# A fused attention, gated-MLP and channel-mix kernel whose written-out instruction order is drawn up anew

## The chip, the cores and the metric

The kernel runs on one core of one Trainium2 chip. The metric is the device time of one execution in microseconds (us), lower is better. Times are of single executions; the profiled execution is one of them, with every instruction recorded.

## What is computed

Three layers follow each other, on 4 batches of 576 tokens:

```python
# attention: 8 heads of 64, with a decay from the running sum of log f
scores = q @ k.T / 8 + cum[:, None] - cum[None, :]      # causal
x = softmax(scores) @ v                                  # -> (4, 576, 512)
# gated MLP with a spatial product over the tokens
h = relu(x @ w_in); u, v = h[..., :512], h[..., 512:]
v = (v - mean) / sqrt(var + 1e-6)
x = (u * (w_spatial @ v + b_spatial)) @ w_out
# channel mix with the token before
k = relu((mu_k*x + (1-mu_k)*x_prev) @ w_k)
r = sigmoid((mu_r*x + (1-mu_r)*x_prev) @ w_r)
out = r * (k*k @ w_v)
```

## The kernel before

The work on the heads goes by pairs: pair p holds heads 2p and 2p+1 of the 32, so there are 16 pairs, four to a batch. A pair goes through these steps, each a method of class `K`:

- `load`, `qksq`, `qkscale`, `qkhi`, `qklo`: k and q are fetched, scaled and split into a high and a low half-precision part, and transposed by DMA into the tiles kT and qT. `kaux` and `qaux` copy half of them by DMA into kA and qA, where the decay rows are added.
- `score` (tiles s) and `rowmax`: the scores, for the row maxima alone. `mrow` sends the maxima through device memory (md) into two rows of qA.
- `scoreT` (tiles t): the scores again, transposed; ScalarE takes exp into the tile e, GpSimd zeroes the upper triangles (`causal`).
- `products`: `pv` multiplies e by v on 64-column groups of TensorE, `sums` adds e up on 32-column groups; all go to the one tile o in PSUM. `head` copies the numerators into xo.
- `recip`: the sums go to device memory (rd<-sm), come back reshaped (r<-rd), are inverted, and go out and back again (rd<-r, sr<-rd); `norm` multiplies xo by sr on GpSimd, `xhi` and `xlo` split the result into the tile xt of the pair.

When the four pairs of a batch b are there, the MLP of that batch runs: `m1v` (60 matmuls, x by the v half of w_in), `ln1` to `ln4` (normalising it, on ScalarE, VectorE and GpSimd), `m1u` (96 matmuls, the u half) and `m2` (112 matmuls, the spatial product; VectorE multiplies each of its 8 tiles into u, and a DMA sends it to device memory as gd). Each pass over an m1v tile ends with channel block kc = 3, which needs the xt of the batch's last pair. Weights are fetched and converted on the side (`wconv`, `wscale`, `wsplit` for w_in; `weights_spatial`; `early_blocks` for seven blocks of the later weights; `weights2` for the rest).

Then comes the channel mix on chunks of 512 tokens (`m3`, `mix`, `chunk`), a long run of matmuls. Its memory, and the last weights' fetches (mu, w_k, w_r, w_v), use space that the attention's tiles held, so they begin when pair 15 has finished.

All calls up to the last m2 are not issued at once. `Planned` records them, 4,209 in all, and `issue` sends them out in the order of the list `ORDER` (L36), as written in the file; each engine's queue is in that order, and nothing reorders it later. `SLOTS` (L216) fixes for some tiles which of a pool's buffers each use takes. The program that drew up the two tables is not in the file. In the profile L291 is the line of `issue`, so every recorded instruction has that line, and L305 is the line of the calls that come after it. All DMAs but three at the start are issued from one queue, that of SyncE (SP).

Of the kernel before, what the change touches and what calls it, by code (L numbers as in the profile page):

```python
# [36 lines left out]
    0, 2, 234, 1, 4, 961, 3, 6, 235, 5, 49, 7, 50, 51, 29, 99, 52, 53, 100, 101, 30, 40, 31, 233,  # L37
    41, 102, 103, 32, 245, 33, 253, 269, 277, 291, 301, 305, 34, 8, 9, 10, 11, 42, 12, 35, 69, 13, 14, 43,
    44, 36, 45, 57, 48, 17, 37, 15, 71, 54, 16, 18, 19, 38, 72, 59, 20, 55, 61, 21, 62, 22, 73, 46,
    63, 23, 26, 24, 28, 84, 25, 56, 39, 27, 60, 64, 85, 65, 74, 47, 86, 90, 91, 67, 87, 222, 92, 88,  # L40
    68, 95, 75, 93, 70, 89, 96, 108, 76, 58, 107, 109, 94, 66, 104, 78, 128, 79, 80, 110, 106, 111, 112, 81,
    113, 97, 114, 82, 77, 98, 138, 139, 115, 122, 105, 123, 124, 125, 126, 127, 132, 133, 141, 134, 130, 131, 129, 146,
    147, 142, 136, 218, 148, 149, 143, 144, 150, 186, 152, 232, 121, 153, 145, 154, 151, 155, 156, 157, 160, 158, 161, 162,
    268, 163, 159, 164, 165, 172, 168, 166, 169, 170, 294, 167, 171, 173, 174, 320, 175, 176, 391, 177, 179, 392, 137, 393,
    394, 395, 140, 396, 180, 184, 181, 188, 135, 397, 189, 187, 185, 223, 206, 178, 207, 190, 191, 192, 193, 182, 194, 199,
    183, 231, 219, 195, 200, 201, 202, 221, 203, 204, 205, 247, 214, 215, 216, 209, 196, 229, 248, 210, 197, 378, 249, 211,
    220, 250, 198, 83, 334, 212, 407, 319, 236, 251, 208, 386, 237, 238, 213, 255, 331, 256, 257, 217, 258, 259, 260, 224,
    225, 226, 239, 227, 240, 241, 252, 242, 261, 228, 243, 278, 279, 280, 262, 281, 244, 282, 283, 230, 263, 264, 310, 284,
    265, 266, 302, 303, 304, 286, 246, 267, 287, 285, 288, 289, 295, 290, 306, 270, 296, 311, 271, 312, 297, 292, 298, 293,
    299, 300, 313, 307, 308, 323, 324, 327, 314, 309, 332, 328, 329, 333, 325, 335, 317, 336, 337, 417, 330, 338, 339, 340,  # L50
    326, 343, 344, 345, 117, 116, 346, 341, 347, 348, 349, 416, 426, 350, 351, 342, 352, 315, 118, 353, 354, 355, 387, 356,
    357, 358, 119, 445, 380, 381, 382, 359, 383, 446, 384, 385, 360, 403, 447, 404, 405, 361, 389, 120, 415, 364, 448, 390,
    365, 515, 316, 449, 366, 408, 367, 450, 362, 368, 369, 272, 428, 423, 273, 429, 430, 525, 363, 451, 452, 453, 454, 425,
    455, 456, 274, 436, 467, 275, 457, 468, 469, 470, 495, 471, 276, 472, 458, 473, 321, 370, 371, 1151, 409, 474, 400, 398,
    401, 514, 505, 1152, 496, 475, 497, 498, 573, 372, 528, 519, 520, 522, 521, 501, 402, 580, 418, 388, 419, 420, 534, 421,
    535, 442, 406, 536, 537, 592, 506, 538, 539, 540, 437, 438, 524, 439, 422, 440, 507, 541, 574, 441, 575, 576, 424, 577,
    410, 578, 579, 459, 460, 499, 542, 461, 444, 462, 476, 477, 411, 478, 583, 479, 463, 412, 508, 484, 509, 584, 480, 510,
    485, 465, 322, 466, 486, 644, 481, 487, 482, 399, 488, 489, 670, 502, 503, 516, 517, 588, 589, 590, 443, 612, 601, 613,
    614, 504, 526, 518, 543, 527, 512, 544, 545, 689, 546, 593, 500, 523, 602, 628, 629, 630, 631, 632, 633, 615, 547, 548,
    706, 549, 581, 550, 551, 634, 552, 553, 611, 554, 555, 635, 556, 557, 558, 675, 749, 645, 646, 647, 511, 648, 649, 650,  # L60
    622, 413, 667, 668, 559, 669, 798, 623, 651, 560, 561, 414, 624, 799, 652, 564, 565, 625, 600, 800, 671, 683, 566, 626,
    801, 567, 676, 627, 568, 802, 569, 610, 677, 697, 570, 608, 571, 585, 694, 562, 586, 572, 678, 690, 254, 691, 679, 587,
    603, 744, 582, 604, 605, 680, 606, 464, 698, 563, 699, 607, 616, 617, 618, 2133, 803, 619, 318, 620, 636, 637, 638, 591,
    639, 2134, 483, 653, 609, 654, 804, 655, 656, 640, 692, 621, 700, 701, 693, 702, 703, 1153, 513, 657, 1154, 672, 704, 673,
    738, 739, 740, 674, 741, 742, 743, 705, 685, 686, 661, 771, 642, 687, 696, 643, 662, 772, 695, 663, 747, 658, 373, 664,
    374, 659, 665, 666, 748, 781, 753, 754, 755, 1155, 682, 375, 707, 681, 688, 708, 709, 594, 710, 763, 376, 711, 712, 745,
    713, 714, 715, 431, 716, 432, 717, 718, 719, 377, 720, 433, 721, 722, 734, 595, 770, 434, 735, 723, 750, 724, 751, 379,
    736, 596, 782, 783, 784, 597, 752, 807, 746, 808, 785, 809, 810, 811, 812, 773, 774, 725, 775, 813, 756, 776, 435, 780,
    786, 787, 788, 789, 814, 823, 777, 726, 824, 825, 826, 852, 827, 828, 845, 846, 790, 847, 792, 727, 829, 728, 779, 729,
    793, 830, 737, 730, 791, 731, 794, 427, 732, 733, 848, 795, 815, 853, 816, 778, 796, 875, 817, 762, 818, 831, 832, 833,  # L70
    819, 854, 834, 797, 868, 923, 869, 855, 598, 839, 835, 821, 856, 822, 840, 599, 491, 862, 836, 841, 857, 842, 490, 837,
    872, 764, 843, 844, 849, 850, 864, 865, 870, 851, 924, 876, 492, 866, 877, 878, 859, 879, 880, 945, 881, 867, 884, 871,
    885, 886, 493, 887, 888, 889, 890, 891, 892, 873, 882, 494, 893, 894, 874, 895, 896, 897, 898, 883, 899, 529, 917, 530,
    918, 919, 920, 921, 900, 922, 944, 931, 932, 531, 933, 901, 902, 926, 905, 954, 903, 906, 532, 907, 908, 904, 909, 927,
    910, 533, 971, 641, 972, 858, 936, 955, 765, 956, 957, 977, 978, 979, 980, 981, 953, 982, 757, 660, 758, 964, 943, 759,
    766, 999, 684, 760, 1000, 1001, 767, 1002, 1003, 1004, 911, 937, 912, 928, 913, 929, 983, 1156, 1157, 951, 761, 984, 1158, 925,
    946, 947, 948, 2375, 949, 1392, 930, 1028, 2376, 768, 1021, 1393, 1022, 1023, 1005, 950, 938, 965, 934, 966, 967, 769, 1006, 968,
    805, 939, 985, 952, 1024, 986, 940, 973, 987, 988, 1029, 1048, 969, 974, 916, 1030, 1049, 806, 1031, 935, 989, 1007, 970, 1008,
    1032, 1009, 1051, 1010, 1036, 1033, 1067, 991, 1068, 1069, 992, 1070, 1025, 1026, 975, 1055, 1015, 1011, 820, 941, 1052, 1016, 1027, 1017,
    860, 942, 1108, 1018, 914, 1019, 1020, 1012, 1045, 1046, 1104, 1013, 1071, 1105, 1130, 838, 1106, 1035, 1107, 1073, 1053, 1054, 1074, 1075,  # L80
    1047, 863, 958, 1076, 1072, 976, 1170, 1131, 1171, 1118, 1119, 1034, 1050, 1140, 1172, 1111, 1109, 990, 1077, 861, 1078, 1079, 1080, 1081,
    1082, 1112, 1083, 1084, 1085, 915, 1086, 1087, 1014, 1088, 1129, 1160, 1122, 1100, 959, 960, 1101, 1089, 962, 1037, 1115, 1090, 1116, 1102,
    1161, 1141, 963, 1162, 1142, 1117, 1166, 1167, 1110, 1168, 1169, 1132, 1133, 1145, 1134, 1091, 1139, 1135, 1120, 1146, 1147, 1148, 1136, 1163,
    1149, 1176, 1092, 1196, 1197, 1198, 1199, 1150, 1164, 1173, 1093, 1177, 1138, 1174, 1165, 1175, 1200, 1252, 1178, 1103, 1159, 1179, 1293, 1180,
    1181, 1202, 1121, 1203, 1189, 1201, 1204, 1205, 1232, 1233, 1190, 1290, 1191, 1182, 1192, 1193, 1209, 1206, 1194, 1184, 1195, 1185, 1235, 1236,
    1277, 1361, 1237, 1272, 1207, 1273, 1225, 1408, 1274, 1208, 1226, 1227, 1251, 1210, 1291, 1228, 1280, 1234, 1211, 1292, 1229, 1230, 1212, 1213,
    1295, 1238, 1245, 1244, 1214, 1246, 1239, 1247, 1215, 1248, 1257, 1249, 1362, 1216, 1250, 1217, 1266, 1258, 993, 1267, 1275, 1268, 1269, 1270,
    1259, 1271, 1276, 1261, 1283, 1284, 1260, 1123, 1285, 1289, 994, 1286, 1262, 1287, 1263, 1288, 1282, 1264, 1278, 1296, 1265, 1297, 1281, 1298,
    1308, 995, 1309, 1310, 1299, 1311, 996, 1312, 1313, 1316, 1240, 1350, 997, 1351, 1241, 1352, 1300, 1314, 1242, 1353, 1301, 1354, 1317, 1303,
    1355, 1407, 1315, 1356, 1302, 1357, 1360, 1358, 998, 1359, 1386, 1387, 1304, 1375, 1417, 1376, 1305, 1377, 1124, 1349, 1306, 1364, 1378, 1243,  # L90
# [1169 lines left out]
```

## Time and profile before

| | us |
|---|---|
| median of 3 runs (lowest to highest) | 718.86 (715.58 to 720.31) |
| the profiled execution | 720.54 |
| its span, first to last instruction | 718.8 |
| TensorE (PE) busy | 655.2 (91%) |
| weight loads (PEld) busy | 466.8 (65%) |
| VectorE (DVE) busy | 426.7 (59%) |
| ScalarE (ACT) busy | 372.1 (52%) |
| GpSimd (POOL) busy | 142.9 (20%) |

The span is read in stages: up to 24 us the first tiles are loaded and prepared; up to 112 us come pairs 0 to 4 with hardly any MLP work; up to 348 us attention and the MLPs of batches 0 to 2; up to 413 us the last products of attention and the MLP of batch 3; then the channel mix. TensorE's granted clock is given as a share of full speed, 1.00 for 2.4 GHz and 0.50 for 1.2 GHz.

### The profile page before, as it was taken

To read this page: it belongs to the slowest core of one execution; us is meant where nothing else is said; L and a number is where in the kernel's file an instruction comes from. 1 tells how busy PE (TensorE), PEld (TensorE's weight loads), DVE (VectorE), ACT (ScalarE), POOL (GpSimd) and SP (SyncE) were. 2 spreads that over 40 slices of the span, in tenths; PEclk is the share of its full clock that TensorE was granted. 3 is DMA by queue.
4 is the path that set the end of the run, shared out by engine and by line. 5 is a ranking of instruction groups with operands and counts; after the bars stand their busy time and mean duration, and the time that the engine had idled before them with its cause. 6 is when DMAs were issued, how large, how long until landed. Compare 5 with 4: busy or idle time off the path is not lost.

```text
span 718.8 us, 11708 instructions
## 1 busy us (share of the span) xinstructions
PE 655.2 (91%) x4238; PEld 466.8 (65%) x4238; DVE 426.7 (59%) x1077; ACT 372.1 (52%) x765; POOL 142.9 (20%) x343
## 2 busy tenths in 40 slices
PE   0598988999889999999858899999999999999997
PEld 0254544667545775557525687888888888888896
DVE  6778869896848946533139789465135413632351
ACT  5568857873678705564137478363236224532431
POOL 7023436501356303460115000000000000000000
PEclk9999979999999999999969999999999999999999
DMA  6887858646578324201133644011010100100010
GB/s 207 222 206 217 209 111 208 199 95 171 156 169 197 74 97 94 68 25 35 51 106 117 197 143 138 30 30 59 1 45 0 59 0 16 51 9 1 1 59 29
DMA packets 73615, 70.06 MB, mean 97 GB/s; under 512 B 50883, under 2 KB 51555, under 8 KB 73558
## 3 DMA queue, kind: packets, MB, share of 16 engines
q1 hardware_dynamic: 73126, 68.14, 35.2%
q10 hardware_dynamic: 432, 1.18, 0.5%
q8 instruction: 33, 0.54, 0.3%
q14 instruction: 24, 0.20, 0.1%
HBM read 43.78 MB, written 9.79 MB: 75 GB/s over the span
## 4 chain that ended last, share of the span: by engine, by line
PE 63%; DVE 12%; DMA 10%; ACT 5%; POOL 5%; issue 3%; SPq 2%; DVEq 0%; POOLq 0%; ACTq 0%
PE m L305 40%; PE m1u L291 4%; PE o L291 4%; PE s L291 4%; PE m L291 4%; PE t L291 4%; PE m1v L291 3%; SPq L291 2%; DMA sr<-rd 2%; ACT e L291 2%; DVE nm L291 2%; DMA wst<-in_moe_w_k_dram 1%; POOL xo L291 1%; POOL mv L291 1%; DVE wf L291 1%
## 5 line engine op out<-in xcount | busy, mean ns | idle before, releaser
L305 PE MATMUL m<-xx,moe_w_k 128*128 128x512 f32 (+1 forms) x480 | 105.5, 369 | 0.0
L305 PE MATMUL m<-moe_w_v,k 128*128 128x512 f32 x432 | 104.0, 390 | 0.0
L305 PEld LDWEIGHTS m<-xx,moe_w_k 128*128 128x128 f32 x480 | 84.0, 188 | 16.1
L305 PEld LDWEIGHTS m<-moe_w_v,k 128*128 128x128 f32 x432 | 80.7, 188 | 17.0
L291 ACT ACTIVATE e<-t,qa 128x512 f32<-128x512 f32 (+1 forms) x128 | 71.0, 593 | 28.8 <-PE t L291 20.9
L291 POOL TENSOR_SCALAR_AFFINE_SELECT e<-e 128x128 f32<-128x128 f32 (+1 forms) x160 | 54.5, 361 | 141.4 <-ACT e L291 141.1
L305 DVE TENSOR_TENSOR tmp<-tmp 128x512 f32<-128x512 f32 (+1 forms) x40 | 25.4, 638 | 94.1 <-ACT tmp L305 93.9
L291 PE MATMUL m1v<-win,xt 128*128 128x512 f16 x240 | 60.9, 397 | 12.0 <-ACT xt L291 11.2
L291 PE MATMUL s<-kT,qT 128*128 128x192 f16 (+3 forms) x192 | 55.1, 297 | 17.1 <-DMA qT<-nq 7.4
L305 ACT ACTIVATE tmp<-m 128x512 f32<-128x512 f32 (+1 forms) x40 | 22.3, 557 | 79.2 <-PE m L305 78.6
L305 PE MATMUL m<-gh,moe_w_out 128*128 128x512 f32 (+1 forms) x240 | 55.8, 382 | 2.8 <-DVE u L291 2.0
L291 DVE CUSTOM_DVE_ANT_0 junk<-s,mask 128x512 bf16<-128x512 f32 (+4 forms) x100 | 47.4, 474 | 13.5 <-PE s L291 9.9
L291 PE MATMUL m1u<-xt,win 128*128 128x288 f16 x384 | 52.6, 292 | 2.1 <-ACT u L291 2.1
L291 PE MATMUL m<-wspT,vn 128*128 128x288 f16 x384 | 53.3, 286 | 0.2 <-DVE wspT L291 0.2
L291 PE MATMUL s<-kA,qA 67*128 67x192 f16 (+3 forms) x192 | 49.4, 298 | 4.3 <-DMA qA<-qT 4.3
L305 PEld LDWEIGHTS m<-gh,moe_w_out 128*128 128x128 f32 x240 | 43.3, 193 | 12.8 <-DVE u L291 2.3
L291 PE MATMUL o<-e,v 128*64 128x64 f32 (+4 forms) x384 | 50.3, 397 | 1.4 <-ACT xo L291 0.7
L291 PE MATMUL t<-qA,kA 69*128 69x512 f16 (+2 forms) x192 | 48.5, 288 | 3.1 <-ACT e L291 2.7
L305 PE MATMUL m<-moe_w_r,xx 128*128 128x512 f32 x216 | 51.2, 394 | 0.0
L291 PE MATMUL t<-qT,kT 128*128 128x512 f16 (+2 forms) x192 | 50.1, 286 | 0.0
L291 PEld LDWEIGHTS <-xt 128*128 128x128 f16 x240 | 23.0, 101 | 39.6 <-ACT xt L291 11.7
L305 PEld LDWEIGHTS m<-moe_w_r,xx 128*128 128x128 f32 x216 | 40.4, 187 | 9.9
(162 smaller groups left out, 1087.4 us busy)
## 6 DMA issues: line engine op xcount, KB each, us to landing
knat<-in_k_dram SPq DMA_DIRECT2D x16, 320.0 KB
v<-in_v_dram SPq DMA_DIRECT2D x20, 256.0 KB
sr<-rd SPq DMA_DIRECT2D x32, 144.0 KB
gd<-u SPq DMA_DIRECT2D x16, 288.0 KB
out_dram<-o SPq DMA_DIRECT2D x18, 256.0 KB
qnat<-in_q_dram SPq DMA_DIRECT2D x14, 320.0 KB
wst<-in_moe_w_k_dram SPq DMA_DIRECT2D x8, 512.0 KB
g<-gd SPq DMA_DIRECT2D x16, 256.0 KB
```

The lines of the kernel that those rows point to most:

```text
L291: self.tc.keep_in_program_order(fn(*map(now, a), **{x: now(y) for x, y in kw.items()}))
L305: return fn(*map(now, a), **{x: now(y) for x, y in kw.items()})
```

## The change

The numbers in `ORDER` up to the last 30 or so (the m2 products of batch 3 stay where they are), and two rows of `SLOTS` (the buffers of the PSUM pools ps_m and ps_s), are replaced. No operation is added, removed or altered, so every engine does the same work in another order. The tables were drawn up with other rules: the products on column groups (`pv` and `sums`) are ranked together with all other matmuls whose data is there, and a buffer counts as free at the end of its last use.

```diff
 ORDER = [
-    0, 2, 234, 1, 4, 961, 3, 6, 235, 5, 49, 7, 50, 51, 29, 99, 52, 53, 100, 101, 30, 40, 31, 233,
...
+    0, 2, 9, 8, 10, 11, 1, 12, 4, 13, 14, 3, 6, 5, 7, 17, 15, 16, 29, 18, 30, 19, 20, 40,
...
-    ('ps_m', 'm'): [0, 1, 0, 0, 0, 1, 1, 1, 0, 0, 0, 0, 0, 1, 0, 0, 1, 0, 1, 0, 1, 0, 0, 1,
...
+    ('ps_m', 'm'): [0, 1, 0, 1, 1, 0, 0, 1, 0, 0, 0, 0, 1, 1, 1, 0, 1, 0, 1, 0, 1, 1, 0, 0, 1,
...
```

First place: TensorE, the end of the sums of pair 15, the last pair, and what comes behind them. In the names o holds a pair's sums and numerators, ones is the tile that sums, m1v the v half of batch 3, xt_142 and xt_144 the normalised outputs of pairs 14 and 15. Before:

```order
L291 MATMUL o<-e,ones 32x192 x2
L291 LDWEIGHTS xt_142
L291 MATMUL m1v<-win,xt_142 128x512
L291 LDWEIGHTS xt_142
L291 MATMUL m1v<-win,xt_142 128x512
L291 LDWEIGHTS xt_142
L291 MATMUL m1v<-win,xt_142 128x512
L291 MATMUL o<-e,v_616 64x320 x2
L291 MATMUL o<-e,v_616 64x192 x2
L291 MATMUL o<-e,v_616 64x64 x2
L291 LDWEIGHTS xt_144
```

and now, where vn is the normalised v half of batch 2, and m_4418 the first tile of its spatial product:

```order
L291 MATMUL o<-e,ones 32x192 x2
L291 LDWEIGHTS vn
L291 MATMUL m_4418<-wspT,vn 128x288
L291 LDWEIGHTS vn
L291 MATMUL m_4418<-wspT,vn 128x288
L291 LDWEIGHTS vn
L291 MATMUL m_4418<-wspT,vn 128x288
L291 LDWEIGHTS vn
L291 MATMUL m_4418<-wspT,vn 128x288
L291 LDWEIGHTS vn
L291 MATMUL m_4418<-wspT,vn 128x288
L291 LDWEIGHTS vn
```

Before, all 112 m2 matmuls of batch 2 and six m1v matmuls of batch 3 stand ahead of these sums, three m1v matmuls and the last pv behind them, and then the first matmul that needs pair 15 (xt_144). Now the 112 m2 matmuls and nine m1v matmuls stand between the sums and the first use of pair 15.

Second place: the SP queue at the end of pairs 14 and 15. rd, r and sr are the stations of `recip`, gd<-u sends out the gated tiles of batch 2, mu is the first transfer of the channel mix. Before:

```order
L291 DMA rd_4352<-r_4326 128x9
L291 DMA sr<-rd_4352 64x576 x2
L291 DMA gd<-u 128x576 x4
L291 DMA rd_4568<-sm 2x384
L291 DMA rd_4568<-sm 2x192
L291 DMA r_4578<-rd_4568 128x9
L291 DMA rd_4582<-r_4578 128x9
L291 DMA sr<-rd_4582 64x576 x2
L291 DMA mu<-in_moe_mu_k_dram 128x4
```

and now:

```order
L291 DMA rd_4381<-r_4365 128x9
L291 DMA sr<-rd_4381 64x576 x2
L291 DMA rd_4436<-sm 2x384
L291 DMA rd_4436<-sm 2x192
L291 DMA r_4458<-rd_4436 128x9
L291 DMA gd<-u 128x576
L291 DMA rd_4484<-r_4458 128x9
L291 DMA sr<-rd_4484 64x576 x2
L291 DMA gd<-u 128x576 x2
L291 DMA mu<-in_moe_mu_k_dram 128x4
```

The four gd transfers stood ahead of pair 15's first rd; now the first of them stands between its r and its second rd, two stand behind sr, and the last comes later still.

Third place: the SP queue near the start, around pair 1. knat and qnat are raw k and q of pairs 2 and 3, wst is a block of w_in, kT, qT, kA and qA are of pair 1, md is pair 0's row of maxima. Before:

```order
L291 DMA qnat_254<-in_q_dram 128x640
L291 DMA v_257<-in_v_dram 128x512 x5
L291 DMA kA_108<-cumd 3x1280
L291 DMA_TRANSPOSE kT_104<-nk 128x10x128
L291 DMA_TRANSPOSE qT_293<-nq 128x10x128
L291 DMA knat_91<-in_k_dram 128x640
L291 DMA md<-mr 20x128
L291 DMA kA_108<-kT_104 64x1280
L291 DMA qA_263<-qT_293 64x1280
```

and now:

```order
L291 DMA qnat_256<-in_q_dram 128x640
L291 DMA wst<-in_moe_w_in_dram 128x1024
L291 DMA v_262<-in_v_dram 128x512 x5
L291 DMA_TRANSPOSE kT_157<-nk 128x10x128
L291 DMA_TRANSPOSE qT_285<-nq 128x10x128
L291 DMA kA_162<-cumd 3x1280
L291 DMA knat_95<-in_k_dram 128x640
L291 DMA qnat_87<-in_q_dram 128x640
L291 DMA md<-mr 20x128
L291 DMA kA_162<-kT_157 64x1280
L291 DMA qA_260<-qT_285 64x1280
```

Block 3 of w_in (wst) now stands ahead of v and of pair 1's transposes, and q of pair 3 (the second qnat) ahead of pair 1's qA<-qT; before, both came behind it.

## Rows read from the trace of the kernel before

**Rows 1.** Busy time by engine in stages; us, engine busy (count), granted clock, DMA share, GB/s.

```profile
24.00:112.00 88.00, 74.57 (x618) 42.60 (x616) 71.11 (x212) 60.84 (x133) 29.50 (x56) 0.94 0.76 189
112.00:348.00 236.00, 226.34 (x1903) 143.84 (x1903) 159.47 (x503) 139.99 (x312) 83.60 (x209) 1.00 0.48 121
348.00:413.00 65.00, 49.83 (x340) 30.83 (x337) 37.73 (x75) 31.01 (x64) 15.02 (x29) 0.87 0.39 121
440.00:719.00 279.00, 274.98 (x1267) 227.21 (x1265) 116.13 (x212) 106.49 (x195) 0.58 (x3) 1.00 0.08 27
```

**Rows 2.** What TensorE waited for over the span: total us, times, longest.

```profile
PE m1v L291 <- ACT xt L291: 11.2, 3, 10.2
PE s L291 <- DVE nm L291: 7.1, 11, 1.5
```

**Rows 3.** Timeline 348 to 369 us, all engines: start, us, instruction [idle before <- releaser].

```profile
351.55 1.95 PE L291 MATMUL o<-e,v 128*64 128x512 f32 x12 [0.74 <-ACT xo L291]
...
353.42 1.61 PE L291 MATMUL o<-e,ones 128*32 128x192 f32 x32
...
355.97 1.20 PE L291 MATMUL o<-e,v 128*64 128x320 f32 x12 [0.19 <-ACT sm L291]
...
360.12 0.33 SPq L291 DMA_DIRECT2D rd<-r  x1
...
365.21 1.40 POOL L291 TENSOR_TENSOR xo<-xo,sr 128x576 f32<-128x576 f32 x1 [10.16 <-DMA sr<-rd]
...
367.37 1.04 PE L291 MATMUL m1v<-win,xt 128*128 128x512 f16 x2 [10.20 <-ACT xt L291]
367.39 1.27 POOL L291 TENSOR_TENSOR xt<-xo,xt 128x576 f16<-128x576 f32 x1 [0.78 <-ACT xt L291]
368.69 0.34 SPq L291 DMA_DIRECT2D mu<-in_moe_mu_k_dram  x1
...
368.72 13.24 PE L291 MATMUL m1v<-win,xt 128*128 128x512 f16 x49 [0.32 <-POOL xt L291]
```

**Rows 4.** The chain that ended last, around 340 us: start, us, what.

```profile
334.67 13.72 PE m L291 x112
348.39 1.29 PE m1v L291 x6
```

**Rows 5.** Stretches of half clock; columns as in rows 1.

```profile
93.90:104.10 10.20, 8.68 (x37) 4.42 (x38) 4.98 (x27) 4.17 (x8) 2.16 (x4) 0.50 0.34 69
...
367.30:373.80 6.50, 6.11 (x14) 1.94 (x15) 3.52 (x8) 5.12 (x11) 1.27 (x1) 0.50 0.51 130
390.90:394.30 3.40, 3.40 (x16) 2.15 (x15) 3.31 (x7) 2.72 (x8) 2.00 (x5) 0.50 0.00 0
```

**Rows 6.** Timeline of TensorE, 380 to 442 us.

```profile
381.80 6.04 PE L291 MATMUL m1u<-xt,win 128*128 128x288 f16 x48
389.96 7.71 PE L291 MATMUL m1u<-xt,win 128*128 128x288 f16 x48 [2.12 <-ACT u L291]
...
413.38 13.00 PE L305 MATMUL m<-gh,moe_w_out 128*128 128x512 f32 x48 [1.99 <-DVE u L291]
```

**Rows 7.** Timeline of TensorE, some waits between 30 and 115 us.

```profile
35.22 0.56 PE L291 MATMUL s<-kA,qA 67*128 67x448 f16 x1 [2.67 <-DMA qA<-qT]
...
94.56 0.61 PE L291 MATMUL s<-kT,qT 128*128 128x512 f16 x1 [1.53 <-DVE nm L291]
97.90 0.45 PE L291 MATMUL s<-kT,qT 128*128 128x320 f16 x1 [0.85 <-DVE sw L291]
110.21 0.85 PE L291 MATMUL o<-e,ones 128*32 128x192 f32 x8 [1.59 <-POOL e L291]
```

**Rows 8.** The stretch of the first loads; columns as in rows 1.

```profile
24.00:44.00 20.00, 14.58 (x80) 8.38 (x79) 14.90 (x46) 9.46 (x22) 1.52 (x3) 1.00 0.95 238
```

**Rows 9.** Stretches of mostly attention; columns as in rows 1.

```profile
180.00:200.00 20.00, 18.05 (x178) 10.30 (x176) 15.66 (x67) 13.20 (x28) 8.30 (x16) 1.00 0.56 147
200.00:220.00 20.00, 17.99 (x146) 9.65 (x143) 12.43 (x34) 15.82 (x38) 10.15 (x22) 1.00 0.80 192
```

352 rows, old and new, of tables (ORDER, SLOTS) are left out of this document.

## The prediction, made before the changed kernel ran

> **What bounds the kernel now.** The first view is the busy time by stage [rows 1]. TensorE is busy for 226.34 of 236 us from 112 to 348 us and for 274.98 of 279 us after 440 us: there its own work is the bound, and no order can win more than the gaps, 9.7 and 4.0 us. Two stages are looser. From 24 to 112 us it is busy for 74.57 of 88 us, a gap of 13.4 us; from 348 to 413 us for 49.83 of 65 us, a gap of 15.2 us. The change moves nothing after the last m2 products, so the question is what it does to these two gaps and whether it opens others.
>
> The second view, TensorE's waits, names the largest: m1v waited for xt, once for 10.2 us of 11.2 in all [rows 2]. The second in that list, s waiting for the row maxima, is eleven small waits, 7.1 us together.
>
> The third view, the timeline around that wait, shows where it comes from [rows 3]. The sums of pair 15 start at 353.42 and take 1.61 us, so they end at 355.03. What follows is a chain of copies and transfers that TensorE has no part in: r goes out again at 360.12, sr is back and the normalising starts at 365.21, the high part of xt frees the next m1v matmul at 367.37, and the low part is done at 367.39 + 1.27 = 368.66. That is 13.6 us behind the sums. TensorE had only three m1v matmuls and the last pv (1.20 us) to do in that time. The space of the attention's tiles is free then too: mu, the first transfer of the channel mix, goes at 368.69.
>
> **The change at the end of attention.** Before these sums TensorE did the 112 m2 matmuls of batch 2 in 13.72 us and six m1v matmuls of batch 3 in 1.29 us [rows 4]; none of these needs pair 15. In the new order they stand behind the sums. So, measured against all that comes earlier, the sums of pair 15 start 13.72 + 1.29 = 15.0 us sooner. One wait of 0.74 us, of pair 15's pv for the tile o [rows 3], goes as well, since m1u matmuls now stand between the pairs' products.
>
> Is the chain covered then? Behind the sums stand the 112 matmuls (13.72 us), the last pv (1.20 us) and nine m1v matmuls at 1.29 / 6 = 0.215 us (1.94 us): 16.9 us, against 13.6 us of chain. The chain gets longer, though. On the SP queue the first gd stands between r and the second rd. It waits for the second m2 tile of batch 2: 28 of the 112 matmuls (3.4 us) and the pv (1.2 us) behind the sums, then VectorE's product, so some 5.4 us, while the second rd used to go 360.12 - 355.03 = 5.1 us behind the sums. With the gd's own issue, and up to three transfers of gd in flight beside sr, I add 1.5 us, between 0.5 us and 3 us. The chain is 15.1 us, still under 16.9 us.
>
> How much of the 15.7 us reaches the end? There are two ways to count. By the chain: all that waits for pair 15, the weights of the channel mix included, comes 15.0 + 0.7 - 1.5 = 14.2 us earlier. By TensorE: the waits of 10.20, 0.74, 0.32 and 0.19 us [rows 3] make 11.45 us, and the half clock that follows goes too. From 367.30 to 373.80 the granted clock was 0.50, the 1.2 GHz level, and TensorE was busy for 6.11 us [rows 5]; at full clock half of that is left, so 3.1 us. Together that is 14.5 us. The two agree.
>
> The wait of 2.12 us at the second half of m1u [rows 6] I leave in. It is for ScalarE, whose work from the end of pair 15 on (weight conversions, ln steps) took until 389.96 - 368.66 = 21.3 us behind it; counted from the sums that is 15.1 + 21.3 = 36.4 us now. TensorE would be there after 16.9 us, 51 m1v matmuls (11.0 us) and 48 of m1u (6.04 us, rows 6), at 33.9 us, so it waits about as before, and the half clock after it (3.40 us at 0.50, so 1.7 us, rows 5) may stay. If both went, the gain would be 14.5 + 2.1 + 1.7 = 18.3 us. The wait of 1.99 us before the channel mix stays: m3 follows the same last m2 product. For this place I take -14.5 us, between -18.3 and -9.
>
> The clock rule bears on this. The rows show half clock behind the wait of 10.20 us, and also behind those of 2.12 us [rows 5, 6] and 1.53 us [rows 5, 7]. The Trainium skill (TensorE: Matmul & The Clock Gate, Part 1) says that the half-rate clock is the default and sustained activity lifts it, so that work in place of a wait also saves the slow matmuls after it. By that rule the 3.1 us belong to the gain, without it the sum would be 11.4 us here; the trace agrees with it at these three places.
>
> **The change up to 112 us.** One edit costs. Pair 1's qA<-qT, for which TensorE waited 2.67 us at 35.22 [rows 7], now has a w_in block of 512 KB and a q of 320 KB ahead of it that came behind it. In this stretch the DMA engines are busy for 0.95 of the time and move 238 GB/s [rows 8]; 832 KB at that rate take 3.5 us. Nothing else is ready for TensorE there. I count +3. Other edits help. The scale of the v half of w_in is taken among the scores of pair 0, where engines still wait for loads, no longer among those of pair 2; the one of the u half moves forward likewise (the wait of 0.85 us, sw, rows 7, was for it). The normalising of pair 2 no longer stands between the triangles of pair 4, whose sums waited for GpSimd for 1.59 us. These are 2.4 us, and an even chance of losing the dip at 93.9 to 104.1, where 8.68 busy us at 0.50 [rows 5] cost 4.3, would give some more. I take 0 for the stage; the ends are -12 (nearly all of the 13.4 us gone) and +6 (the transfers, and new waits of the size of the old ones in rows 7).
>
> **The change from 112 to 348 us.** The order now mixes m1v, m1u and m2 matmuls with every pair's scores and products. Before, MLP work came in blocks, with attention nearly alone between. In such a stretch, 180 to 220 us, TensorE lost 1.95 + 2.01 us of 40 [rows 9]; in the blocks it lost next to nothing. Cover for each chain of a pair grows on average, but the last pv and sums of several pairs now stand closer behind the exp and triangles that they need. Gaps are 9.7 us now; at best they vanish, at the worst the density of 180 to 220 us holds throughout, 236 x 0.099 = 23.4 us, which is +14. I take -3, a third of the gaps, nearer to the best since the waits of rows 9 stem from the lumps.
>
> **The sum.** -14.5 + 0 - 3 = -17.5. The profiled execution took 720.54 us (span 718.8 and 1.7 around it), so 703.0; the median of the runs is 1.7 below that execution. I predict 702.
>
> **Rivals.**
> - *The waits move into the last pairs.* Pairs 13 to 15 now follow each other with less MLP work between exp and products than the batch-2 block gave them. If each of six late pairs waits 1.4 us more (the first wait at 180 to 220 us summed to 4 us for three pairs), 8.4 us come back: 711 to 716, within 1% of before. For it: the sums of pair 15 stand 9 us of matmuls behind those of 14. Against it: m1u matmuls stand between all of them, and all waits from 112 to 348 us together are 9.7 us now [rows 1].
> - *The early stage tightens as well.* TensorE's busy time from 24 to 112 us holds waits inside the chains of short matmuls: weight loads take 42.60 of 88 us there and 143.84 of 236 us later [rows 1]. At the later density (0.61) the same loads would take 70 us, 18 us less; with the tail that gives 684. For it: this is the loosest stretch. Against it: it waits for loads and for row maxima, and pair 1's transfers come later. The Trainium skill (Trainium Kernel Development and Optimization, Performance Expectations) says that matmul busy time is a bad measure and weight-load time a good one; by that rule this stretch, not the tail, has the most to give.
> - *Slower: the clock.* Kinds of matmul change more often on TensorE now, each change a place for a short wait, and waits of 1.53 to 2.12 us were followed by half clock. A dip as from 93.9 to 104.1 costs 4.3 us [rows 5]. From the sixth such dip on (26 us) the tail's 14.5 us and the 3 us are lost and 1% more: 727 or above. For it: three such dips are in rows 5. Against it: from 112 to 348 us the granted clock is 1.00 throughout [rows 1], waits included.
> - *The order does not do what it says*: buffers free too late by the real clock. Then products wait for o or for s as at 351.55; this is the first rival with the same price.
>
> **Chances.** The forecast (690 to 708) 0.74; the early stage too (680 to 690) 0.07; waits in the last pairs (708 to 718) 0.15; slower by the clock 0.04. A measurement of this kernel can tell about 1% from no change, so 711.7 and 726 are the marks: of the third case a fifth is faster by over 1%. Faster: 0.74 + 0.07 + 0.03 = 0.84; within 1%: 0.12; slower: 0.04. The range that leaves 2 in 10 out reaches 690 to 714.
>
> **What would show it.** Right: m1v of batch 3 waits under 2 us for xt; the last sums come about 15 us earlier than 353.4, and the channel mix starts near 396 to 400 us; full clock from there to m1u; a wait of some 2 us for ScalarE at m1u remains. The early term is right if TensorE's wait for pair 1's qA ends near 38 us. Wrong: m1v still waits 5 us or more for pair 15; or the sums of pair 15 end after 350 us because TensorE waited elsewhere, which would show as gaps of over 13 us from 112 to 340 us, or as stretches of half clock there.

## The result, and the profile after

The changed kernel takes 707.09 us in the median of 4 runs (705.93 to 709.21), the kernel before 718.45 on the same chip: a ratio of 0.985, 95% interval 0.981 to 0.989, or 11.4 us less. The forecast was 702, between 690 and 714. Measured again beside the experiments it took 705.92 (6 runs; 0.983, from 0.980 to 0.987).

The profiled execution took 705.93 us (span 703.9), 14.6 us under that of before. That is more than the medians differ, because before's profiled execution lay 2.1 us above its median and this one lies 1.2 us below. So 3 us of what the two traces show apart belongs to the two executions, not to the kernels.

First the timeline of the stretch on which the forecast rested, 333 to 400 us (start, us, instruction, idle before and what ended it):

```profile
333.85 1.61 PE L291 MATMUL o<-e,ones 128*32 128x192 f32 x32
...
340.27 0.52 DVE L291 SCALAR_TENSOR_TENSOR u<-m,sw,u 128x288 f32<-128x288 f32 x1 [2.43 <-PE m L291]
340.70 0.22 DVE L291 TENSOR_SCALAR r<-r,sv 128x9 f32<-128x9 f32 x1
340.81 0.33 SPq L291 DMA_DIRECT2D gd<-u  x1
...
341.23 0.38 SPq L291 DMA_DIRECT2D rd<-r  x1
343.29 1.13 SPq L291 DMA_DIRECT2D sr<-rd  x2
...
347.19 1.41 POOL L291 TENSOR_TENSOR xo<-xo,sr 128x576 f32<-128x576 f32 x1 [7.33 <-DMA sr<-rd]
...
349.38 1.28 POOL L291 TENSOR_TENSOR xt<-xo,xt 128x576 f16<-128x576 f32 x1 [0.78 <-ACT xt L291]
350.69 0.33 SPq L291 DMA_DIRECT2D mu<-in_moe_mu_k_dram  x1
...
371.68 6.04 PE L291 MATMUL m1u<-xt,win 128*128 128x288 f16 x48 [2.33 <-ACT u L291]
...
392.95 0.33 SPq L305 DMA_DIRECT2D wst<-in_moe_w_v_dram  x1
...
397.36 0.43 DVE L305 TENSOR_SCALAR wst<-wst 128x512 int32<-128x512 int32 x1 [2.70 <-DMA wst<-in_moe_w_v_dram]
397.70 0.51 DVE L291 SCALAR_TENSOR_TENSOR u<-m,sw,u 128x288 f32<-128x288 f32 x1
...
398.27 7.08 PE L305 MATMUL m<-gh,moe_w_out 128*128 128x512 f32 x18 [5.53 <-DVE u L291]
```

Beside [rows 3] and [rows 6]: the sums of pair 15 start 19.6 us earlier (353.42 before), the low part of xt ends 18.0 us earlier (350.66, 368.66 before), and m1v waits no longer for it. Not all of the 19.6 us is the change: run 1 below, whose order up to pair 14 is the old one, has these sums at 331.96. But the channel mix (m3) starts only 15.1 us earlier (413.38 before). From the end of xt to m3 it took 44.7 us, now 47.6: 2.9 us are given back. The last row says where one looks: m3 waits 5.53 us for VectorE's last gate product (1.99 in [rows 6]), and the rows above it say why that is late: in VectorE's queue a conversion of w_v stands ahead of it, and waits for its load. In the trace of before two of them stood there already, behind a load that came back sooner:

```profile
407.83 0.33 SPq L305 DMA_DIRECT2D wst<-in_moe_w_v_dram  x1
...
411.43 0.43 DVE L305 TENSOR_SCALAR wst<-wst 128x512 int32<-128x512 int32 x1 [1.19 <-DMA wst<-in_moe_w_v_dram]
...
412.20 0.69 DVE L305 SCALAR_TENSOR_TENSOR we<-we,wst 128x512 int32<-128x512 int32 x1 [0.35 <-ACT we L305]
412.81 0.51 DVE L291 SCALAR_TENSOR_TENSOR u<-m,sw,u 128x288 f32<-128x288 f32 x1
```

The stages, with the columns of [rows 1], and the stretch of half clock behind that wait:

```profile
24.00:112.00 88.00, 74.60 (x635) 41.87 (x635) 70.66 (x216) 62.63 (x136) 25.27 (x57) 0.97 0.71 181
112.00:348.00 236.00, 228.85 (x1942) 143.25 (x1935) 152.29 (x503) 142.22 (x314) 86.55 (x210) 1.00 0.51 123
348.00:413.00 65.00, 56.00 (x341) 39.71 (x340) 48.60 (x92) 36.71 (x73) 10.89 (x27) 0.95 0.49 149
...
397.20:404.00 6.80, 5.73 (x14) 4.48 (x15) 4.89 (x9) 2.04 (x4) 0.00 (x0) 0.50 0.51 169
```

The first stage is as before (74.57 busy). From 348 to 413 us TensorE's busy time rose from 49.83 to 56.00 of 65 us, so the gap shrank by 6.2 us: the 11.45 us of waits for xt and o went, but the wait before m3 grew by 3.5 us and one of 1.1 us in m2 is new. From 112 to 348 us the gaps shrank from 9.7 to 7.2 us. This says little, since the two stretches don't hold the same work: the m2 block of batch 2 lies almost whole in both (from 334.67 before, from 335.39 now), and pair 15's products lie in it only now. What TensorE waited for (total us, times, longest):

```profile
...
PE s L291 <- DVE nm L291: 6.1, 9, 1.6
PE m L305 <- DVE u L291: 5.5, 1, 5.5
PE t L291 <- DMA qA<-md: 5.2, 5, 1.4
...
PE m1u L291 <- ACT u L291: 2.3, 1, 2.3
...
PE m L291 <- ACT u L291: 1.1, 1, 1.1
```

The 11.2 us for xt are gone from the list. New are the waits of t for qA<-md, 5.2 us, nearly all between 160 and 310 us.

### The profile page after: what moved, and what is told of

Its sections match the earlier page's. It is cut to its first block, busy times and chain, and to the rows that moved or that the text cites. A ratio compares the mean times of both kernels' runs of the same rounds, so it can differ in the third digit from the quotient of the medians.

```text
span 703.9 us, 11693 instructions
## 1 busy us (share of the span) xinstructions
PE 649.9 (92%) x4238; PEld 463.2 (66%) x4238; DVE 418.8 (59%) x1077; ACT 373.0 (53%) x765; POOL 136.9 (19%) x343
## 3 DMA queue, kind: packets, MB, share of 16 engines
q10 hardware_dynamic: 432, 1.18, 0.5%
## 4 chain that ended last, share of the span: by engine, by line
PE 64%; DVE 11%; DMA 10%; ACT 5%; POOL 3%; issue 3%; SPq 3%; POOLq 0%; DVEq 0%; ACTq 0%
PE m L305 43%; PE o L291 5%; PE t L291 4%; PE s L291 3%; PE m1u L291 3%; PE m L291 3%; SPq L291 3%; DMA qA<-md 2%; PE m1v L291 2%; DVE nm L291 1%; DMA v<-in_v_dram 1%; POOL mv L291 1%; DVE junk L291 1%; ACT junka L291 1%; DMA g<-gd 1%
## 5 line engine op out<-in xcount | busy, mean ns | idle before, releaser
L305 PE MATMUL m<-xx,moe_w_k 128*128 128x512 f32 (+1 forms) x480 | 105.5, 369 | 0.0
L305 PE MATMUL m<-moe_w_v,k 128*128 128x512 f32 x432 | 104.3, 390 | 0.0
L305 PEld LDWEIGHTS m<-xx,moe_w_k 128*128 128x128 f32 x480 | 83.9, 188 | 16.2 <-ACT tmp L305 0.2
L305 PEld LDWEIGHTS m<-moe_w_v,k 128*128 128x128 f32 x432 | 80.7, 188 | 17.1
L305 DVE TENSOR_TENSOR tmp<-tmp 128x512 f32<-128x512 f32 (+1 forms) x40 | 25.4, 638 | 92.9 <-ACT tmp L305 92.7
L291 POOL TENSOR_SCALAR_AFFINE_SELECT e<-e 128x128 f32<-128x128 f32 (+1 forms) x160 | 50.5, 330 | 130.6 <-ACT e L291 129.9
L291 DVE CUSTOM_DVE_ANT_0 junk<-s,mask 128x320 bf16<-128x320 f32 (+4 forms) x100 | 47.5, 475 | 29.4 <-PE s L291 27.0
L305 ACT ACTIVATE tmp<-m 128x512 f32<-128x512 f32 (+1 forms) x40 | 22.3, 557 | 78.7 <-PE m L305 77.9
L305 PE MATMUL m<-gh,moe_w_out 128*128 128x512 f32 (+1 forms) x240 | 57.0, 386 | 5.5 <-DVE u L291 5.5
L291 PE MATMUL m1v<-win,xt 128*128 128x512 f16 x240 | 56.7, 379 | 0.0
L305 PEld LDWEIGHTS m<-gh,moe_w_out 128*128 128x128 f32 x240 | 44.1, 196 | 15.6 <-DVE u L291 5.8
L305 PE MATMUL m<-moe_w_r,xx 128*128 128x512 f32 x216 | 51.2, 394 | 0.0
L305 PEld LDWEIGHTS m<-moe_w_r,xx 128*128 128x128 f32 x216 | 40.4, 187 | 9.9
L291 PEld LDWEIGHTS <-win 128*128 128x128 f16 x384 | 36.2, 98 | 13.4 <-issue 3.1
```

The lines of the kernel that those rows point to most:

```text
L291: self.tc.keep_in_program_order(fn(*map(now, a), **{x: now(y) for x, y in kw.items()}))
L305: return fn(*map(now, a), **{x: now(y) for x, y in kw.items()})
```

## The experiments

All were timed over five rounds beside the kernel before, whose median was 716.99 to 719.10 us there. "Old" and "new" are the orders of before and after. The times in the last four columns are of the one profiled execution each.

| run | median us (runs) | ratio to before, 95% | sums of pair 15 | end of xt | first m3 | span |
|---|---|---|---|---|---|---|
| before | 718.45 (4) | | 353.42 | 368.66 | 413.38 | 718.8 |
| after | 707.09 (4) | 0.985 (0.981 to 0.989) | 333.85 | 350.66 | 398.27 | 703.9 |
| 1 old, block moved | 704.72 (6) | 0.982 (0.978 to 0.986) | 331.96 | 348.51 | 394.15 | 699.4 |
| 2 new, block put back | 717.44 (12) | 0.999 (0.996 to 1.002) | 351.11 | 366.34 | 412.31 | 717.1 |
| 3 new, old behind xt | 704.60 (6) | 0.982 (0.978 to 0.986) | 333.78 | 350.37 | 395.68 | 700.8 |
| 4 new, w_v in order | 700.63 (6) | 0.976 (0.973 to 0.980) | 333.74 | 350.86 | 395.49 | 699.7 |
| after again | 705.92 (6) | 0.983 (0.980 to 0.987) | 331.34 | 348.45 | 395.43 | 700.7 |
| 5 both 3 and 4 | 700.56 (6) | 0.976 (0.972 to 0.981) | 335.88 | 352.55 | 396.33 | 699.0 |
| 6 as 5, early splits moved | 700.21 (6) | 0.976 (0.972 to 0.979) | 331.43 | 348.06 | 393.53 | 696.2 |
| 7 as 5, g split late | 698.54 (6) | 0.974 (0.970 to 0.977) | 334.19 | 351.11 | 392.00 | 694.6 |
| 8 as 7, cover for t | 701.63 (6) | 0.979 (0.975 to 0.982) | 342.02 | 358.59 | 400.76 | 703.4 |
| 9 as 7, old attention | 697.05 (6) | 0.971 (0.967 to 0.976) | 337.81 | 354.42 | 397.36 | 700.0 |
| 10 as 7, cover at the right pairs | 694.94 (7) | 0.968 (0.964 to 0.971) | 335.65 | 352.18 | 395.47 | 698.1 |
| 11 as 10, two waits mended | 692.67 (6) | 0.967 (0.964 to 0.970) | 332.01 | 348.44 | 387.88 | 690.5 |

In the diffs rows of `ORDER` are written as the operations that they stand for.

**1. The old order with the block moved.**

```diff
 PE  last m1u of batch 2
-PE  m2 of batch 2 x112, m1v of batch 3 x6
 PE  pv of pair 14, pv of pair 15 part 0, sums of pair 15
+PE  m2 of batch 2 x14, pv of pair 15 part 1, m2 x98, m1v of batch 3 x9
```

> The kernel before, with one block moved: the 112 m2 matmuls of batch 2 (with their gate products and gd transfers) and six m1v of batch 3 stand behind the sums of pair 15, as in the changed kernel; every row up to there and every row behind xt as before. Theory 1 (the tail alone is the gain): sums of pair 15 start 15 us earlier than 353.4, near 338 to 339, no wait of m1v for xt above 2 us, the channel mix starts near 399 to 400, total 13 to 15 us under the kernel before, near 704. Theory 2 (the reordering of attention up to 348 us carries most of it): total within 4 us of the kernel before, above 714, because other waits come in at the same place.

704.72: 14.0 us under before (10 to 16 by the interval). Up to pair 14 this kernel's order is word for word the old one. The sums, with those of pair 14 in front:

```profile
317.59 1.61 PE L291 MATMUL o<-e,ones 128*32 128x192 f32 x32
...
331.96 1.60 PE L291 MATMUL o<-e,ones 128*32 128x192 f32 x32
```

From one to the other it is 14.4 us here; before it was 29.3 (324.13 to 353.42). The difference, 14.9 us, is the 15.0 us of matmuls moved. Counted from the start of the span the sums came at 331.96, not at the 338 to 339 expected: up to pair 14 this execution was faster than that of before with the same order, and run 9, with that order once more, has them at 337.81. Theory 1 holds: the one block carries the whole gain. That its median lies 1.2 and 2.4 us under the two of the changed kernel is within the intervals.

**2. The new order with the block put back.**

```diff
+PE  m2 of batch 2 x112, m1v of batch 3 x6
 PE  sums of pair 15
-PE  m2 x14, pv of pair 15 part 1, m2 x98, m1v of batch 3 x9
+PE  m1v of batch 3 x3, pv of pair 15 part 1
```

> The changed kernel, with the same block put back ahead of the sums of pair 15; rows up to the last pv of part 0 and behind xt stay as changed. Theory 1: sums of pair 15 at 348 to 349, m1v waits for xt some 9 to 11 us again, total 12 to 15 us over the changed kernel, 719 to 722, so the rest of the new order is worth about nothing. Theory 2: total 711 or less, the rest of the order keeps its gain of 7 us or more. If the two parts add up, this run and the run with the tail alone lie symmetrically about the mean of before and after.

717.44, not to be told from before (0.996 to 1.002), and m1v waits for xt as long as in [rows 3]:

```profile
365.05 1.03 PE L291 MATMUL m1v<-win,xt 128*128 128x512 f16 x2 [10.20 <-ACT xt L291]
```

So the rest of the new order, from the first load to the last conversion, is worth 1.3 us, with zero inside the interval. The two runs do not add up: 14.0 + 1.3 is 15.3, the full change brought 11.4 and, the second time, 13.2. Each of these numbers is good to some 3 us only, so the 2 to 4 us between them may be nothing. The trace shows where to look all the same, behind xt, and that the 1.3 us already hold a loss there. With the block put back, m3 waits as long for the last gate product as in the changed kernel:

```profile
412.31 7.92 PE L305 MATMUL m<-gh,moe_w_out 128*128 128x512 f32 x25 [5.83 <-DVE u L291]
```

With the new order behind xt this wait is 5.53, 4.67 and 5.83 us (after, after again, run 2), with the old one 1.99, 1.32 and 2.38 (before, run 1, run 3). It goes with the order behind xt, then, and not with the block.

**3. The new order up to xt, the old one behind it.**

```diff
-rows of ORDER from the last m1v of part 0 on: as in the kernel after
+rows of ORDER from the last m1v of part 0 on: as in the kernel before
```

> The changed kernel up to xt of pair 15; everything behind it in the order of the kernel before (weight conversions of the channel mix, ln steps, m1u and m2 of batch 3). From the end of xt to the first matmul of the channel mix it took 44.7 us before and 47.6 after. Theory W (the third and fourth w_k conversions stand later in the new order and pull w_r and w_v with them): 44.5 to 45.5 us here, total 2 to 3 us under the changed kernel, near 704.5. Theory G (g comes back from DRAM late because three gd transfers are still under way beside the weights, whatever the order): 47 us or more, total within 1 us of 707.

704.60. TensorE's queue is that of the changed kernel; only the other engines' orders differ. From xt to m3 it takes 45.3 us, where the changed kernel's two executions have 47.6 and 47.0, and the fourth load of w_k goes 19.1 us behind xt and not 25.4: theory W, by the trace. The times, against 707.09 and 705.92, point the same way, but their intervals overlap. Against run 1 (704.72), which differs from it only in the order up to xt and its buffers, there is no difference: by this pair the new order of attention is worth 0.1 us, give or take 4.

**4. w_v's conversions kept behind the last gate product.**

```diff
-    w2b = k.weights2(k.p2, ("moe2_w_v",), wst)
+    w2b = k.weights2(k.p2, ("moe2_w_v",), wst, True)
```

> The changed kernel, with the conversions of w_v kept in program order, so that on VectorE the last gate product of batch 3 stands ahead of the first of them, which waits for its load. Theory D (that load is what the channel mix waits for, through VectorE's order): the wait before the first m3 matmul falls from 5.5 to under 2.5 us, it starts at 394.5 to 396 instead of 398.3, the half clock of 397.2 to 404.0 shrinks or goes, total 3 to 6 us under the changed kernel, 701 to 704. Rival (something else of the channel mix is as late: w_out, gh, or w_k, w_r and w_v later on, now that their conversions start later): the wait moves to another operand or into the channel mix, total within 1 us of 707, or over it.

```profile
394.50 0.94 DVE L291 SCALAR_TENSOR_TENSOR u<-m,sw,u 128x288 f32<-128x288 f32 x2
...
395.49 6.71 PE L305 MATMUL m<-gh,moe_w_out 128*128 128x512 f32 x21 [2.10 <-DVE u L291]
```

The wait falls to 2.10 us, m3 starts 44.6 us behind xt and not 47.6, and from m3 to the end it takes 304.2 us, not 305.6. The median is 700.63, just past the good end of theory D (701 to 704); its interval lies under the changed kernel's first and overlaps the second by a hair. This call, like all calls of L305, isn't recorded in `ORDER`, so the statement that nothing reorders a queue holds only for the recorded calls: nothing in the file fixed the place of the w_v conversions among them. The first had come to stand directly ahead of the product that m3 needs (397.36 and 397.70 above).

**The changed kernel again, and 5. both edits.**

> The changed kernel itself once more, beside the next three, as the mark for them: 705 to 709 us. Its sums of pair 4 start between 107.5 and 110.5 and its sums of pair 15 between 333.5 and 336 if single executions differ by as much as the kernels with the same order did (107.69 to 110.37 for pair 4).

> The changed kernel with both edits behind xt: the order of the kernel before there, and the conversions of w_v kept behind the last gate product on VectorE. If the two causes of the 2.9 us given back are separate and both real: the wait before the first m3 falls under 1 us (2.38 with the first edit alone, 2.10 with the second alone), 43 to 44.5 us from xt to m3, total 698 to 701. Rival (the weight chain is the bound by now, so what is won before m3 is lost in the channel mix): the time from m3 to the end grows from 304 to 306 or more, total 702 to 705.

The changed kernel repeats (705.92; pair 4 at 108.59, pair 15 at 331.34, some 2 us earlier than I had allowed). With both edits m3 waits only 0.61 us for u (2.38 and 2.10 with one of them), and m3 to the end takes 302.7 us, so nothing is lost in the channel mix. Run 6, with the same order behind xt, has the same two numbers. It starts m3 43.8 us behind xt, but run 6 does so at 45.5, so that step is within what single executions differ by. The median, 700.56, is that of run 4: what the old order behind xt adds to w_v in order shows in this wait and not in the times.

**6. The early splits.**

```diff
-ACT  wsplit 1, 2, 3 of w_in
 ACT  qksq of pair 3: k, q
+ACT  wsplit 1, 2, 3 of w_in
```

> As the run with both edits, and three w_in splits on ScalarE (with VectorE's part of them) moved behind the squares of pair 3's q, early in the kernel. In the changed kernel TensorE waits 2.57 us at 38.77 for the totals of pair 3's scale. Theory A (those squares stood behind the three splits, 1.93 us): that wait falls under 1 us and the sums of pair 4 start 1.5 to 2.5 us earlier than in the run with both edits, total 1 to 2.5 us less. Rival (that wait only hides the next one, for row maxima or for t's qA): the wait goes, the sums of pair 4 move by less than 1 us, total the same within 1 us.

```profile
36.61 0.58 PE L291 MATMUL tot<-qa,ones 128*128 128x2 f32 x2 [1.18 <-ACT junka L291]
...
39.67 0.58 PE L291 MATMUL t<-qA,kA 69*128 69x512 f16 x1 [1.50 <-DMA qA<-md]
```

The wait for the totals falls from 2.57 to 1.18 us, and the next t waits 1.50 us for qA<-md, where it had waited for nothing. The sums of pair 4 start at 108.61 (108.65 in run 5), the median is the same: the rival. That wait covered another.

**7. The splits of g put later.**

```diff
+    m3 = k.m3(0)
+    next(m3)
     k.nc.issue()
...
-    for _ in k.m3(0):
+    next(w2, 0)
+    for _ in m3:
         next(w2, 0)
...
-ACT, DVE  g split wherever the scheduler had room
+ACT, DVE  g split behind the ln steps of batch 3, as rows of ORDER
```

> As the run with both edits, and the four splits of g for the channel mix put later on ScalarE and VectorE, behind the ln steps of batch 3: in the changed kernel ScalarE stands idle 4.4 us in front of the first of them, with ln1 of batch 3 queued behind, and TensorE then waits 2.33 us for ScalarE's u, followed by m1u matmuls at half clock. Theory A (that idle time is the cause of the m1u wait): the wait falls under 1 us, the 48 m1u matmuls take 6.0 us and not 7.7, total 2 to 4 us under the run with both edits, 695 to 698. Rival (the ln chain of small steps between ScalarE, GpSimd and VectorE is as long by itself, or the late splits hold m3 back): the m1u wait stays at 2 us or more, or a wait of over 2 us for gh appears before m3; total within 1 us of the run with both edits.

In run 4 ScalarE's queue still reads as in the changed kernel:

```profile
360.18 1.27 ACT L305 CAST gh<-g 128x512 fp32r<-128x512 f32 x2 [4.46 <-DMA g<-gd]
361.36 0.68 ACT L291 ACTIVATE v<-m1v,ds 128x512 f32<-128x512 f32 x1
```

The second row is ln1 of batch 3: its m1v tile was full by about 355.4 us (24 matmuls of 0.215 us from 350.24), and it stood behind the split, which waited for a transfer. With the splits later, the 96 m1u matmuls run without a stop, at full clock:

```profile
363.64 11.92 PE L291 MATMUL m1u<-xt,win 128*128 128x288 f16 x96
```

In the changed kernel the second 48 of them took 6.04 us in the one execution and 7.71 in the other, behind waits of 2.33 and 2.49 us. The wait at m1u is gone, and m3 starts 40.9 us behind xt (42.2, 42.9 and 43.3 in runs 8 to 10, which keep this tail). The median is 698.54: 2.0 us under run 5, the low end of theory A (it misses the 695 to 698 by half a us), with intervals that overlap.

**8. and 10. Cover for the new waits of t.** Run 8 was to put work in front of the t matmuls that wait for qA<-md. Its blocks stood at pairs 8, 10, 11, 12 and 14 (not at 9, as the expectation of run 10 has it), and the waits are those of pairs 7, 9, 10, 11 and 14: the two longest, 1.86 and 1.15 us, were not touched.

```diff
 PE  sums
-PE  t, pv or m1v, m1u, m2 block
+PE  pv or m1v, m1u, m2 block, t
```

> As the run with both edits and the late splits of g (698.54), and in five places of the new attention order, where the first t of a pair waits for qA<-md (1.86 at 160.47, 1.15 at 201.87, 0.69 at 219.77, 1.02 at 244.25, 0.68 at 308.69, together 5.4 us), the MLP and pv matmuls that stood right behind those t matmuls are put in front of them. Theory A (these waits are what the new order lost again of the 3 us forecast for 112 to 348 us): they fall under 1.5 us together, sums of pair 15 start 3 to 5 us earlier, near 330, total 694 to 696. Rival (they only stand for the next wait of the pair: t and then pv and sums come later by what was put in front, and TensorE waits for exp, triangles or the tile o instead): t waits go, others of 3 us or more come in from 160 to 340 us, sums of pair 15 within 2 us of 334, total 697 to 700.

701.63, the rival or worse. A pv moved up to the sums ran into a wait of its own, for ScalarE's copies out of the tile o:

```profile
226.56 1.20 PE L291 MATMUL o<-e,v 128*64 128x320 f32 x12 [1.88 <-ACT sm L291]
```

Run 10 does it at the right five pairs and moves no pv:

> As the run with both edits and the late splits of g (698.54). The last attempt put its blocks at pairs 8, 9, 10, 12 and 14, while the five waits of t for qA<-md are those of pairs 7, 9, 10, 11 and 14 (1.86, 1.15, 0.69, 1.02 and 0.68 us, the first two at pairs 7 and 9), and one of its blocks held a pv that had to wait for ScalarE's copies of the sums. Here scores, MLP matmuls and one total of a later pair stand in front of the first t at exactly these five places, and no pv is moved. Theory A (these waits are what the new order lost of the 3 us forecast for 112 to 348 us): the five fall under 1.5 us together, sums of pair 15 start 3 to 5 us earlier than 334.19, total 694 to 696. Rival (what fills one wait opens the next, because each pair's exp, triangles and pv follow t in a chain as long as before): t's waits for qA go, sums of pair 15 start within 1.5 us of 334.19, total 697.5 or more.

694.94, the total of theory A, 3.6 us under run 7 (ratios 0.968 and 0.974; their intervals just overlap). t's waits for qA<-md fell from 5.9 to 1.5 us, those for exp rose from 2.2 to 4.4. The trace by itself doesn't show the gain: its execution was the slowest of the seven (699.86, the others up to 696.05), with half clock at 110, 226 and 386 us, and its sums of pair 15 come at 335.65, not 3 to 5 us before 334.19.

**9. The old attention with the new tail.**

```diff
-rows of ORDER up to pair 14: as in the kernel after
+rows of ORDER up to pair 14: as in the kernel before
```

> The kernel before, its own order of attention to the end of pair 14, with the moved block (m2 of batch 2 behind the last sums), w_v's conversions behind the last gate product, and the late splits of g. It differs from the run with both edits and late splits in nothing but the new order of attention and of the early stage. If that order is worth what I forecast (0 to 112 us: 0, 112 to 348 us: -3 us), this run comes out at 701 to 702. If it is worth nothing, it comes out at 698 to 699 like that run. If the new order costs time, 694 to 697.

697.05, beside 698.54 for run 7: the intervals overlap, so by this pair the new order of attention gains nothing that the times can show; the medians even lean the other way, by 1.5 us.

**11. The two waits that run 10 opened.** In front of one t three m1v matmuls stand instead of six, and two g splits go to ScalarE earlier.

> As the run before (694.94), with two waits of its profile mended: in front of pair 10's first t only three m1v matmuls, not six (its later t waited 1.71 us for exp at 224.43), and the first two splits of g on ScalarE right behind the last ln1 of batch 3 and the last two loads of g earlier, so that ScalarE no longer waits 2.54 us for g with a u behind it (an m2 matmul of batch 3 waited 2.28 us for that u, at 386.17). Theory A: both waits fall under 0.8 us, no half clock from 226 to 229 and 386 to 389 us, total 692 to 694. Rival (the mended run already gets no more than chance out of these places, the dips of its one profiled execution being rare): total 694 to 696.

```profile
PE t L291 <- ACT e L291: 3.5, 8, 1.1
PE t L291 <- DMA qA<-md: 2.2, 4, 0.7
PE m L305 <- DVE u L291: 0.8, 1, 0.8
```

692.67, the fastest of all (0.967, 0.964 to 0.970). The wait for exp is 1.07 us, not under 0.8; that of m2 is gone. m3 starts 39.4 us behind xt. Whether the last 2.3 us against run 10 are real the intervals don't tell.

## Why the prediction was right, and where it was not

- **The block behind the last sums, forecast -14.5.** Right, mechanism and size. Alone it brings -14.0, and taking it away gives 717.44. The sums moved by 14.9 us of the 15.0 (run 1). The half clock of [rows 5] behind the wait for xt went too: in the trace of after the clock is full from 114 to 396 us (in the second one it falls once before the channel mix, to 0.50 at 370 us, behind the wait at m1u), and in run 2, with the wait back, it is at or near 0.50 from 358 to 368. The Trainium skill (TensorE: Matmul & The Clock Gate, Part 1) says that the half-rate clock is the default and activity lifts it; the trace agrees.
- **The chain from sums to xt, 15.1 us.** The size was right (335.46 to 350.66 is 15.2), the reason only in part. I had put the 1.5 us down to the gd ahead of the second rd on SP. That gd goes at 340.81 and rd at 341.23, so it held little. What came late is r: its row shows no wait for its transfer, but begins as VectorE ends a gate product (340.27), which itself had waited for its m2 tile. From r's issue to its use it took 2.22 us, 1.56 before; from rd to sr 2.06 and not 1.47; for sr to land 3.90 and not 3.62. Together these are the 1.5 us.
- **"The wait of 2.12 us at m1u I leave in."** Right, 2.33 us. Its cause, though, was not ScalarE's amount of work but one instruction in its queue, the split of g that waits for a transfer (run 7).
- **"The wait of 1.99 us before the channel mix stays: m3 follows the same last m2 product."** This is the step that failed. m3 follows the last gate product on VectorE, and that stands behind a conversion of w_v. The trace of before showed it (411.43 to 412.81 above): the load came in just as the last m2 tile was done, and most of the 1.99 us went to two conversions (run 5, with none ahead, waits 0.61). In the new order that load goes 42.3 us behind xt (392.95) and not 39.2 (407.83), since the fourth block of w_k is loaded later: 25.4 us behind xt, 18.9 before, 23.3 in run 2 with the new order there, 19.1 in run 3 with the old. g comes back later too (first used 9.3 us behind xt, 8.2 before), but run 1 has that as well (9.4) without the long wait. So the wait grew to 5.53 us, 4.67 in the second execution, with 6.8 us of half clock behind it in the first. What the tail won was in part given back here: against 705.92 and 707.09 run 4 has 5.3 and 6.5 us less, since it takes the load out of the product's way altogether. That is more than the 2.9 us by which the way from xt to m3 had grown; from m3 to the end run 4 is 1.2 us shorter than before as well (304.2, 305.4).
- **Up to 112 us, forecast 0.** Right in sum. The sums of pair 4 start at 106.97, 110.21 and 110.75 in three executions of the old order, and between 107.51 and 110.37 in ten of the new (run 6 left out), 108.8 in the mean. The terms did not come as written, so the 0 is in part luck. Pair 1's qA<-qT does go 2.2 us later (34.78, 32.54 before), but TensorE isn't held by it: "nothing else is ready" was wrong, and what ends near 38 us is a wait of 2.57 us for pair 3's totals. Run 6 takes most of that away, and the sums of pair 4 stay. The rival that the early stage tightens had no more to it: weight loads fill 41.87 of 88 us there, 42.60 before. By the rule of the Trainium skill (Trainium Kernel Development and Optimization, Performance Expectations), that weight-load time is a good measure and matmul busy time a bad one, both loose stretches of [rows 1] had room, and not this one before the tail: weight loads fill 0.48 of it and 0.47 of 348 to 413 us. The trace agrees for the tail, where they fill 0.61 now; in the early stretch no run found a gain.
- **From 112 to 348 us, forecast -3.** Mis-sized: -1.3, -0.1 and +1.5 us by runs 2, 3 and 9, each give or take 3 to 4 us, so nearer to nothing, and no run shows the -3. Waits for row maxima went down from 7.1 to 6.1 us, and t's waits for qA<-md, 5.2 us, came in. The premise that cover "grows on average" does not hold for this chain: counted in `ORDER`, a pair from 5 to 15 has 47 matmuls between `mrow` and its first t, 49 before. Of the five pairs that wait for qA<-md, pairs 7, 9, 10 and 14 have fewer than before, and pair 11 has more. That these waits were the loss, run 10 makes likely.
- **The rivals.** No wait of a us stands in the last pairs, the clock is 1.00 from 114 to 396 us, and the order does what it says.
- **Two slips of the working.** The waits for row maxima are not the second in the list of [rows 2] but the fourth: 8.3 us for `ones` and 7.4 us for qT stand ahead of them, nearly all of it in the first 24 us. And the sum gives 701.3, which was put down as 702. Neither bears on the outcome.

The forecast was -17.5, and 11.4 us came, 13.2 the second time. The block, forecast at -14.5, is worth -14.0. Two things make up the rest: the -3 of attention, which no run shows, and the 2.9 us (2.3 in the second execution) that the way from xt to m3 grew by. That leaves nothing over that these medians could tell.

## What to carry to other kernels

Work that needs nothing of the last result belongs behind the last producer, in front of the first consumer; move that block alone and time it before a whole order is drawn up anew. When a chain gets shorter, follow the next one to its last wait, and look at the instruction that stands ahead of the named releaser in its queue: one that waits for a load costs all that is behind it. A wait closed at one place counts only if the next wait of the same chain doesn't open.

## What the runs showed of the hardware that I had not expected

One order of instructions does not give one trace. Of the six executions with the new order unaltered from pair 4 to pair 15 and the block moved (after, after again, runs 3, 4, 5, 7), this stretch took from 222.8 to 227.2 us. Runs 1 and 9 have the old order of before up to pair 14, and differ at 94 us. In run 1:

```profile
94.38 0.39 PE L291 MATMUL s<-kT,qT 128*128 128x512 f16 x1 [0.32 <-DVE nm L291]
...
94.00:104.00 10.00, 8.41 (x59) 4.55 (x60) 7.88 (x34) 7.50 (x15) 4.67 (x9) 1.00 0.59 134
```

and in run 9, like [rows 5] and [rows 7] of before:

```profile
95.32 0.61 PE L291 MATMUL s<-kT,qT 128*128 128x512 f16 x1 [1.35 <-DVE nm L291]
...
94.00:104.00 10.00, 7.83 (x34) 4.04 (x35) 5.02 (x24) 3.31 (x7) 1.86 (x3) 0.55 0.30 66
```

The same instruction waits 0.32 or 1.35 us, and ten us at full or at half clock follow, some 4 us of the time. Nor does the size of a wait decide: t waited 1.86 us at 160.47 in run 7, and the pv behind it ran at full clock; in run 8, with 1.93 us at 160.22, it ran at half:

```profile
161.93 1.20 PE L291 MATMUL o<-e,v 128*64 128x320 f32 x12
```

```profile
161.76 2.19 PE L291 MATMUL o<-e,v 128*64 128x320 f32 x12
```

The Trainium skill (TensorE: Matmul & The Clock Gate, Part 1) says that the number of slow matmuls at the start differs from run to run of one kernel. These traces show such a difference in the middle, with 0.55 and 1.00 for the same ten us of one order. So a single pair of traces here is good to some 4 us, and the medians over five rounds had to carry every step smaller than that.
